# The first unit of a clustered-attention kernel: the second head's choice of clusters in pieces between the first steps

## The chip, the cores and the metric

One core of one Trainium2 chip runs the whole program. The time is that of the device for one execution, in microseconds (us); the kernel before was run three times and profiled once. TensorE is called PE, VectorE DVE, ScalarE ACT, GpSimd POOL; SP (SyncE) issues most transfers.

## What is computed

Attention in which a query sees only the keys of its own cluster, then a mixture of experts, then a dense layer, all in float32 with 2 x 8 heads, 768 positions and head size 64:

```python
q_assign = argmax(q_n @ c_n.T)          # 16 centroids for each head, rows normed
k_assign = argmax(k_n @ c_n.T)
mask = q_assign[:, :, :, None] == k_assign[:, :, None, :]
scores = scale * (q @ k.T); scores = where(mask, scores, -1e9)
attn = exp(scores - max) / (sum + 1e-9);  x = attn @ v
# mixture of experts: 1536 tokens, width 512, 8 experts of 1024
# dense: width 512 -> 2048 -> 512, h * sigmoid(1.702 h)
```

## The kernel before

The attention goes over 8 units (a batch and a pair of heads each). A unit has 12 steps: two heads of six blocks of 128 queries. The steps of all units make one list, and the loop over `i` emits them as a pipeline, in program order, which is the order that each engine keeps: scores of step i + 1 on PE (`emit_scores`, L425 and L426, four matmuls of 384 columns into a buffer `sp`, of which there are two) with their row maximum on DVE (L428), then the transposes of step i - 1 (`emit_pt`, six on PE at L442; ACT copies the high part, L446, DVE the low part, L447), a part of the product with V (L464, L465), and the exponential of step i + 1 on ACT (L434).

Float32 numbers are split into a high and a low part, so each score is a product of stacked rows: Q1 and X hold high parts twice and high with low, and Q2 and Z hold low and high parts in rows 0 to 63 and the one-hot cluster of each position in rows 64 to 79, with a large penalty. Scores of a head so need the choice of its clusters: a product with the centroids, a chain of maxima and comparisons, a transpose of the one-hot, and a copy into rows 64 to 79 of Q2 and Z.

For units 1 to 7 this preparation is cut into nine pieces, which `prep_pieces` returns and `plan_at` hangs on steps of the unit before: 0 and 1 transpose q of the two heads (L244, with the high part on ACT at L247 and the low on DVE at L248), 2 and 3 the same for k; 1 and 3 also issue the copies into the stacks on SP (L262, six of 192 KB each); 4 and 5 are the products with the centroids for q and k (L274, L275, reduced at L277), 5 also starts the choice, of which three instructions run on POOL (L293 to L295); 6 splits v on POOL; 7 ends the choice on DVE (L302, L303), ahead of the step's scores; 8 transposes the one-hots (L310), copies them on ACT (L312) and issues four copies on SP (L314, L315). These pieces, the output stage, and the one-hots of unit 0 use the one PSUM buffer `m` of `misc` once the loop is under way. `load_unit` fetches q, k and v of a pair (three transfers of 384 KB) into one of two buffers each.

Unit 0 has versions of its own. Ahead of the loop it chooses the clusters of head 0 (`first["clusters"]`, L351 and L352, twelve matmuls; `first["argmax"]`, L360 to L368, a generator of eight DVE instructions), puts its one-hots straight into Q2 and Z (`first_onehots`: twelve transposes at L380, then four copies at L383 to L386), and does head 1 later: its one-hots go by `first["second"]`, which is the piece 8 for head 1 alone (L310, L312, and two copies on SP). Head 1 is used from step 6. `keep_clock(n)` runs n matmuls of zeros (L135, 512 columns, bf16).

In SP's queue, as in the other engines', an instruction that waits holds those behind it.

Of the kernel before, what the change touches and what calls it, by code (L numbers as in the profile page):

```python
# [13 lines left out]
AF = mybir.ActivationFunctionType  # L14
ALU = mybir.AluOpType
# [12 lines left out]
BIG = float(2 ** 100)  # L28
# [10 lines left out]
def tile_t(j):  # L39

    return 2 * (j % 3) + j // 3
# [3 lines left out]
def attention_moe_ffn(ctx: ExitStack, tc: tile.TileContext, q, k, v, centroids, w_gate, w_og, w1, w2, w_in, w_out, out):  # L45
    nc = tc.nc
# [9 lines left out]
    pen_scale = const.tile([80, 1], F32, name="pen_scale")  # L56
    pen_bias = const.tile([80, 1], F32, name="pen_bias")
# [73 lines left out]
    def keep_clock(n):  # L131

        z = ps_s.tile([128, 2, 512], F32, name="sp", tag="sp")
        for m in range(n):
            nc.tensor.matmul(z[:, m % 2], idle[:, 0:128], idle, start=True, stop=True)  # L135

    def setup_first():
        nc.vector.memset(idle, 0.0)
        keep_clock(5)
        nc.sync.dma_start(out=craw, in_=centroids.rearrange("h c d -> (h c) d"))  # L140
        for h in range(2):
            load_unit(0, "q", h)
            load_unit(0, "k", h)
        make_identity(nc, ident)
        nc.vector.tensor_copy(identb, ident)
        ii = one.tile([128, C], I32, name="ii")
        nc.gpsimd.iota(ii, [[-1, C]], base=C, channel_multiplier=0)
        nc.vector.tensor_copy(rev16, ii)
        nc.vector.memset(pen_scale[0:32], 1.0)
        nc.vector.memset(pen_scale[32:64], BIG)  # L150
        nc.vector.memset(pen_scale[64:80], BIG)
        nc.vector.memset(pen_bias[0:32], 0.0)
        nc.vector.memset(pen_bias[32:64], -BIG)
        nc.vector.memset(pen_bias[64:80], -BIG)
# [21 lines left out]
    def setup_blocks(cnorm):  # L176
        pc = ps_a.tile([128, 512], F32, name="pc", tag="po")
        nc.tensor.transpose(pc[:, :128], cnorm.rearrange("p a d -> p (a d)"), ident)
        src = [pc[64 * r:64 * r + 64, :128].rearrange("p (h c) -> p h c", h=H) for r in range(2)]
        hi = [cblk[64 * r:64 * r + 64, :, r, :] for r in range(2)]  # L180
        for r in range(2):
            nc.scalar.copy(hi[r], src[r])
        for r in range(2):
            nc.vector.tensor_tensor(cblk[64 * r:64 * r + 64, :, 2 + r, :], src[r], f32(hi[r]), op=ALU.subtract)
# [32 lines left out]
    def misc(u, nm):  # L217

        pool, tag = spots[0]
        if len(spots) > 1:  # L220
            spots.append(spots.pop(0))
        return pool.tile([128, 512], F32, name=nm, tag=tag)

    def prep_pieces(u):
# [146 lines left out]
        def first_onehots():  # L371

            flat = d["oh"].rearrange("p t x c -> p (t x c)")
            pts = {}
            for x in (2, 0):
                pt = misc(u, "poh")[0:XW].bitcast(BF16)[:, 0:S]
                pts[x] = pt[64:80]
                for j in range(T):
                    end = (1 + tile_t(j)) * 4 * C + (x + 1) * C
                    nc.tensor.transpose(pt[:, j * 128:(j + 1) * 128], flat[:, end - XW:end], identb)  # L380
            a, b = slice(0, 384), slice(384, S)
            q2, z = d["Q2"][64:80, 0], d["Z"][64:80, 0]
            nc.vector.tensor_scalar(z[:, a], pts[2][:, a], BIG, -BIG, op0=ALU.mult, op1=ALU.add)  # L383
            nc.scalar.activation(z[:, b], pts[2][:, b], AF.Identity, scale=pen_scale[64:80], bias=pen_bias[64:80])
            nc.scalar.copy(q2[:, a], pts[0][:, a])  # L385
            nc.scalar.copy(q2[:, b], pts[0][:, b])  # L386

# [22 lines left out]
    def emit_scores(i):  # L410
        u, h, j = steps[i]
        d = st[u]
        L = live[i] = {}
        if j % 3 == 0:
            L["sm"] = pp.tile([128, 3], F32, name="sm", tag="sm")
            L["pth"] = ptp.tile([128, T, 384], F32R, name="pth", tag="pth")
            L["ptl"] = ptp.tile([128, T, 384], F32R, name="ptl", tag="ptl")
        else:
            for nm in ("sm", "pth", "ptl"):
                L[nm] = live[i - 1][nm]  # L420
        sp = L["sp"] = ps_s.tile([128, 2, 512], F32, name="sp", tag="sp")
        cs = slice(j * 128, (j + 1) * 128)
        for n in range(2):
            ks = slice(384 * n, 384 * n + 384)
            nc.tensor.matmul(sp[:, n, :384], d["Q1"][:, h, cs], d["X"][:, h, ks], start=True, stop=False)  # L425
            nc.tensor.matmul(sp[:, n, :384], d["Q2"][:, h, cs], d["Z"][:, h, ks], start=False, stop=True)  # L426
        nm = L["nm"] = pp.tile([128, 1], F32, name="nm", tag="nm")
        nc.vector.tensor_reduce(nm, sp[:, :, :384], op=ALU.max, axis=AX.XY, negate=True)  # L428

    def emit_exp(i):  # L430
        L = live[i]
        j = steps[i][2]
        P = L["P"] = pp.tile([128, 2, 384], F32, name="P", tag="P")
        nc.scalar.activation(P, L["sp"][:, :, :384], AF.Exp, bias=L["nm"], accum_out=L["sm"][:, j % 3:j % 3 + 1])  # L434
# [222 lines left out]

    plan_at = {}
    for u in range(1, len(UNITS)):
        for n, r in enumerate((-3, -2, 0, 1, 3, 4, 7, 6, 7) if u > 1 else (2, 2, 3, 3, 4, 5, 7, 6, 7)):  # L660
            plan_at.setdefault((12 * (u - 1) + r, n == 7), []).append((u, n))
    pieces = {}

    def prepare(i, early=False):
        for u, n in plan_at.get((i, early), ()):
            if u not in pieces:
                pieces[u] = prep_pieces(u)
            for f in pieces[u][n]:
                f()

    with tc.manual_schedule():
        setup_first()
        first = prep_pieces(0)
        cnorm = setup_centroids()
        first["tr"]("q", 0)()
        first["alloc"]()
        first["tr"]("k", 0)()
        setup_blocks(cnorm)
        first["stacks"](0, "q")()
        first["stacks"](0, "k")()  # L680
        load_unit(0, "v")
        first["tr"]("q", 1)()
        first["tr"]("k", 1)()
        sc = [first["clusters"](0)]
        load_unit(1, "qk")
        chain = [first["argmax"](0, sc[0])]
        for _ in chain[0]:
            pass
        sc.append(first["clusters"](1))
        keep_clock(2)  # L690
        chain.append(first["argmax"](1, sc[1]))
        for _ in range(4):
            next(chain[1])
        first["stacks"](1, "q")()
        first["stacks"](1, "k")()
        first["onehots"]()
        setup_rest()
        first["vsplit"]()
        load_unit(1, "v")
        emit_scores(0)  # L700
        emit_exp(0)
        for i in range(NS + 2):
            if i == 1:
                for _ in chain[1]:
                    pass
            nu, r = divmod(i + 3, 12)
            if i == 3 or r == 0 and nu + 2 < len(UNITS):
                load_unit(nu + 2)
            prepare(i, True)
            if i + 1 < NS:  # L710
                emit_scores(i + 1)
            tail = i >= NS - TAIL
            if (tail or i % 3 == 2) and ost:
                ost.popleft()()
            if i == 1:
                first["second"]()
            prepare(i)
            if i == 0:
                spots[:] = [(ps_m, "m")]
            if i >= 14 and i % 4 == 2 and len(fill) < E:  # L720
                zero_rows(len(fill))
            if i % (NS // 2) == NS // 2 - 5 and i < NS:
                sum_logits(i // (NS // 2))
            if i == NS // 2 + 13:
                routing.append(route(0))
            for _ in range(2 if tail else 1):
                if av:
                    av.popleft()()
            if 0 <= i - 1 < NS:
                emit_pt(i - 1)  # L730
            n = i - (1 if tail else 2)
            if 0 <= n < NS and steps[n][2] % 3 == 2:
                queue_av(n)
            if i + 1 < NS:
                emit_exp(i + 1)
        advance(stop="weighed")
        while av:
            av.popleft()()
        while ost:
            ost.popleft()()  # L740
        advance()
        routing.append(route(2))
        advance()
        finish_routing()
        keep_clock(24)
# [336 lines left out]
    with tc.manual_schedule():  # L1082
# [4 lines left out]
        z = ps_h.tile([128, 512], F32, name="ph", tag="ph")  # L1087
# [17 lines left out]
        for g in range(G + 2):  # L1105
            e, c = divmod(g, 8)
            nxt = wins.get(e + 1)
            r = c - (7 - nxt["nr"]) if nxt else 0
# [76 lines left out]
    with tc.manual_schedule():  # L1185
        gq = deque()
        for g in range(len(seq) + 2):
# [6 lines left out]
            if g >= 2:  # L1194

                for m in range(4) if g < len(seq) or g == len(seq) + 1 else ():
                    for g0, gh, gl in list(gq)[:1] if g < len(seq) else gq:
                        fh, tb, c, i = seq[g0]
# [47 lines left out]
```

## Time and profile before

| | us |
|---|---|
| median of three runs | 778.91 (778.26 to 782.12) |
| the profiled execution | 779.88, of which its span is 778.2 |
| busy PE | 738.0 (95%) |
| busy DVE | 516.3 (66%) |
| busy ACT | 427.4 (55%) |
| busy POOL | 272.7 (35%) |
| mean granted clock of PE | 0.977 of full |

The profile is one execution of the program. Busy times are sums over the whole of it, so they say which engine has most work, not what a stage waits for: for that one reads the same figures by stretches, and the timeline, which lists the instructions in order with the idle time ahead of each and what ended it. The clock is granted at two levels, 1.0 (2.4 GHz) and 0.5 (1.2 GHz); a figure between is a mean over a stretch with both. The attention takes the first 294 us or so of the span; the unit in question, unit 0, its first 55.

### The profile page before, as it was taken

What the parts mean: (1) busy time and instruction counts of PE and PEld (TensorE: products, weight loads), DVE (VectorE), ACT (ScalarE), POOL (GpSimd) and SP (SyncE); (2) the same over time, 40 slices, a digit from 0 to 9 for tenths busy, and PEclk for the clock granted to TensorE, in tenths of its full rate; (3) what the DMA queues carried; (4) which work ended last, traced back from release to release, by engine and by line L of the source; (5) the groups of instructions that cost most, each with busy time, mean ns of one, the idle gap of its engine ahead of it and who ended that gap; (6) DMA issues with size and microseconds to landing.
All of it is one profiled execution on the core that took longest, in us unless ns stands there. A gap on an engine that the chain in (4) does not pass through costs nothing. (4 is left out here: it accounts for less than half of the span.)

```text
span 778.2 us, 12334 instructions
## 1 busy us (share of the span) xinstructions
PE 738.0 (95%) x4355; PEld 653.9 (84%) x4356; DVE 516.3 (66%) x995; ACT 427.4 (55%) x880; POOL 272.7 (35%) x208
## 2 busy tenths in 40 slices
PE   7899999999999995999999999999999999999996
PEld 5789989898898983999989988877888888888885
DVE  6788988989998983445666676786755567342422
ACT  4576867778687861555767777553534335221221
POOL 7022020220372003565767888543521021110101
PEclk7899999999999997799999999999999999999999
DMA  6764749345261004966666876235631121010101
GB/s 167 174 167 143 208 128 274 112 104 132 75 179 33 1 1 154 332 215 207 197 215 219 268 240 222 67 77 104 82 80 55 54 80 56 0 55 1 54 1 54
DMA packets 64608, 97.05 MB, mean 125 GB/s; under 512 B 8832, under 2 KB 42880, under 8 KB 64544
## 3 DMA queue, kind: packets, MB, share of 16 engines
q1 hardware_dynamic: 62240, 89.94, 39.9%
q0 software_dynamic: 2304, 6.30, 2.2%
q8 instruction: 35, 0.57, 0.3%
q14 instruction: 29, 0.24, 0.1%
HBM read 64.46 MB, written 12.59 MB: 99 GB/s over the span
## 5 line engine op out<-in xcount | busy, mean ns | idle before, releaser
L798 POOL TENSOR_TENSOR w<-raw,w 128x1024 fp32r<-128x1024 f32 x47 | 117.5, 2514 | 28.0 <-ACT w L795 25.1
L447 DVE TENSOR_TENSOR ptl<-pt,pth 128x384 fp32r<-128x384 f32 x192 | 98.4, 550 | 24.1 <-ACT pth L446 22.8
L446 ACT CAST pth<-pt 128x384 fp32r<-128x384 f32 x192 | 83.4, 482 | 46.4 <-PE pt L442 45.0
L1153 DVE TENSOR_TENSOR sg<-ph,sg 128x512 f32<-128x512 f32 x48 | 33.2, 692 | 102.8 <-ACT sg L1152 97.3
L434 ACT ACTIVATE P<-sp,nm 128x768 f32<-128x768 f32 x96 | 87.8, 915 | 14.9 <-DVE nm L428 14.3
L428 DVE TENSOR_REDUCE nm<-sp 128x1 f32<-128x768 f32 x96 | 91.0, 948 | 3.2 <-PE sp L426 3.2
L856 POOL TENSOR_TENSOR w<-csq,w 128x512 fp32r<-128x512 f32 x32 | 43.5, 1360 | 136.9 <-ACT w L855 136.9
L1152 ACT ACTIVATE sg<-ph 128x512 f32<-128x512 f32 x48 | 28.6, 597 | 108.2 <-PE ph L1074 107.6
L442 PE MATMUL pt<-ident,P 128*128 128x128 f32 x576 | 82.3, 278 | 0.8 <-DVE ptl L447 0.7
L1170 PE MATMUL py<-w,gl 128*128 128x512 f32 x192 | 75.3, 392 | 2.4 <-DVE gl L1159 2.4
L1073 PE MATMUL ph<-ytl,w 128*128 128x512 f32 x192 | 76.1, 396 | 0.0
L1072 PE MATMUL ph<-yth,w 128*128 128x512 f32 x192 | 75.9, 395 | 0.0
L425 PE MATMUL sp<-X,Q 128*128 128x384 f32 x192 | 74.8, 389 | 0.8 <-ACT P L434 0.8
L1074 PE MATMUL ph<-yth,w 128*128 128x512 f32 x192 | 75.5, 393 | 0.0
L442 PEld LDWEIGHTS pt<-ident,P 128*128 128x128 f32 x576 | 68.5, 142 | 8.2 <-DVE ptl L447 4.8
L1169 PE MATMUL py<-w,gh 128*128 128x512 f32 x192 | 75.3, 392 | 0.0
L1168 PE MATMUL py<-w,gh 128*128 128x512 f32 x192 | 75.0, 391 | 0.0
L464 PE MATMUL po<-pth,vst 128*128 128x384 f32 x192 | 71.3, 371 | 0.0
L795 ACT CAST w<-raw 128x1024 fp32r<-128x1024 f32 x63 | 65.8, 1045 | 4.9 <-DMA raw<-in_moe_w_dram 4.8
L426 PE MATMUL sp<-Z,Q 80*128 80x384 f32 x192 | 66.8, 348 | 1.1 <-ACT Q L385 1.1
L906 PE MATMUL py<-ht,w 128*128 128x480 f32 (+5 forms) x192 | 61.2, 352 | 6.7 <-DVE room L913 4.5
L465 PE MATMUL po<-ptl,vst 128*128 128x384 f32 x192 | 64.8, 338 | 0.0
(232 smaller groups left out, 1746.2 us busy)
## 6 DMA issues: line engine op xcount, KB each, us to landing
raw<-in_moe_w_dram SPq DMA_DIRECT2D x64, 512.0 KB, 3.8
raw<-in_moe_w_in_dram SPq DMA_DIRECT2D x16, 512.0 KB, 3.9
raw<-in_moe_w_out_dram SPq DMA_DIRECT2D x16, 512.0 KB, 4.4
xd<-zrow SPq DMA_DIRECT2D x8, 768.0 KB, 6.4
Q<-Hq SPq DMA_DIRECT2D x28, 192.0 KB, 3.0
ld_v<-in_v_dram SPq DMA_DIRECT2D x8, 384.0 KB, 4.8
xr<-xd SPq DMA_DIRECT2D x6, 512.0 KB, 5.5
ld_q<-in_q_dram SPq DMA_DIRECT2D x7, 384.0 KB, 3.3
```

What stands on the lines that cost most here:

```text
L428: nc.vector.tensor_reduce(nm, sp[:, :, :384], op=ALU.max, axis=AX.XY, negate=True)
L434: nc.scalar.activation(P, L["sp"][:, :, :384], AF.Exp, bias=L["nm"], accum_out=L["sm"][:, j % 3:j % 3 + 1])
L442: nc.tensor.transpose(pt[:, r * 128:(r + 1) * 128], L["P"][:, n, r * 128:(r + 1) * 128], ident)
L446: nc.scalar.copy(hi, src)
L447: nc.vector.tensor_tensor(L["ptl"][:, 3 * n:3 * n + 3, qs], src, f32(hi), op=ALU.subtract)
L798: (eng or nc.gpsimd).tensor_tensor(lo, r, f32(hi), op=ALU.subtract)
L1072: nc.tensor.matmul(ph, wa(key, 0, k, i), yth[:, k, cs], start=(k == 0), stop=False)
L1073: nc.tensor.matmul(ph, wa(key, 0, k, i), ytl[:, k, cs], start=False, stop=False)
L1074: nc.tensor.matmul(ph, wa(key, 1, k, i), yth[:, k, cs], start=False, stop=(k == 3))
L1168: nc.tensor.matmul(po[m], gh[:, ms], wb(key, 0, i), start=first, stop=False)
L1169: nc.tensor.matmul(po[m], gh[:, ms], wb(key, 1, i), start=False, stop=False)
L1170: nc.tensor.matmul(po[m], gl[:, ms], wb(key, 0, i), start=False, stop=last)
```

## The change

Four edits. The copy of the second half of Z's one-hots of head 0 goes from ACT to DVE. The pieces of unit 1 move to other steps: 0 and 1 from step 2 to 1 and 2, 2 and 3 from step 3 to 4 and 5, 4 and 5 from 4 and 5 to 6 and 7, 6 from 7 to 9, 7 from 6 to 8, 8 from 7 to 9. Ahead of the loop the cluster matmuls of head 1, two matmuls of zeros and the first four instructions of head 1's choice give way to fourteen matmuls of zeros; the cluster matmuls come at i = 0 after the scores, and the eight instructions of the choice in twos, threes and fours (three are left for the last) behind the scores' maxima of i = 0, 1 and 2, in place of four ahead of the loop and four at i = 1. The one-hots of head 1 are sent at i = 3 instead of i = 1.

```diff
-            nc.scalar.activation(z[:, b], pts[2][:, b], AF.Identity, scale=pen_scale[64:80], bias=pen_bias[64:80])
+            nc.vector.tensor_scalar(z[:, b], pts[2][:, b], BIG, -BIG, op0=ALU.mult, op1=ALU.add)
...
-        for n, r in enumerate((-3, -2, 0, 1, 3, 4, 7, 6, 7) if u > 1 else (2, 2, 3, 3, 4, 5, 7, 6, 7)):
+        for n, r in enumerate((-3, -2, 0, 1, 3, 4, 7, 6, 7) if u > 1 else (1, 2, 4, 5, 6, 7, 9, 8, 9)):
...
         chain = [first["argmax"](0, sc[0])]
         for _ in chain[0]:
             pass
-        sc.append(first["clusters"](1))
-        keep_clock(2)
-        chain.append(first["argmax"](1, sc[1]))
-        for _ in range(4):
-            next(chain[1])
+        keep_clock(14)
         first["stacks"](1, "q")()
...
         for i in range(NS + 2):
-            if i == 1:
-                for _ in chain[1]:
-                    pass
             nu, r = divmod(i + 3, 12)
             if i == 3 or r == 0 and nu + 2 < len(UNITS):
                 load_unit(nu + 2)
             prepare(i, True)
             if i + 1 < NS:
                 emit_scores(i + 1)
+
+            if i == 0:
+                sc.append(first["clusters"](1))
+                chain.append(first["argmax"](1, sc[1]))
+            for _ in range((2, 3, 4)[i] if i < 3 else 0):
+                next(chain[1], None)
...
-            if i == 1:
+            if i == 3:
                 first["second"]()
             prepare(i)
```

## Rows read from the trace of the kernel before

**Rows 1.** The page's first part: busy time, share of the span, instructions.
```profile
PE 738.0 (95%) x4355; PEld 653.9 (84%) x4356; DVE 516.3 (66%) x995; ACT 427.4 (55%) x880; POOL 272.7 (35%) x208
```

**Rows 2.** Busy time by stretch: stretch and length, engines (instructions), granted clock, DMA, GB/s.
```profile
core 0: us, PE busy (x) PEld busy (x) DVE busy (x) ACT busy (x) POOL busy (x), PEclk, DMA share, GB/s
0.00:50.00 50.00, 40.92 (x233) 34.17 (x234) 35.32 (x81) 27.29 (x58) 20.67 (x50) 0.83 0.62 154
...
46.00:60.00 14.00, 14.00 (x102) 13.65 (x102) 13.45 (x27) 12.12 (x29) 0.00 (x0) 1.00 0.68 184
...
100.00:150.00 50.00, 48.41 (x344) 45.25 (x343) 45.56 (x86) 36.55 (x84) 11.26 (x10) 1.00 0.53 157
```

**Rows 3.** The same view where the granted clock changes.
```profile
8.70:9.00 0.30, 0.30 (x4) 0.30 (x4) 0.30 (x2) 0.00 (x0) 0.30 (x1) 0.53 0.39 92
...
22.30:22.50 0.20, 0.20 (x3) 0.20 (x3) 0.12 (x1) 0.08 (x2) 0.00 (x0) 0.82 0.00 0
...
28.00:30.00 2.00, 1.09 (x6) 1.09 (x7) 0.86 (x2) 0.41 (x2) 0.00 (x0) 0.80 0.95 204
...
32.60:32.80 0.20, 0.20 (x4) 0.20 (x3) 0.20 (x1) 0.00 (x0) 0.00 (x0) 0.97 1.04 277
```

**Rows 4.** Timeline, steps 1 to 3: start, length, engine, line, operation [idle before <-releaser].
```profile
18.54 0.69 PE L425 MATMUL sp<-X,Q 128*128 128x384 f32 x1 [0.79 <-ACT P L434]
18.66 0.57 DVE L366 TENSOR_TENSOR eq<-eq,rev 128x96 f32<-128x96 f32 x2
...
26.04 0.56 DVE L248 SCALAR_TENSOR_TENSOR Lq<-pqk,Hq 128x384 fp32r<-128x384 f32 x1 [1.17 <-ACT Hq L247]
...
26.52 1.01 DVE L447 TENSOR_TENSOR ptl<-pt,pth 128x384 fp32r<-128x384 f32 x2
```

**Rows 5.** Timeline: zeros at the two clocks, and the start up to the first maximum.
```profile
298.58 3.32 PE L135 MATMUL sp<-idle 128*128 128x512 bf16 x14
...
1.26 2.31 PE L135 MATMUL sp<-idle 128*128 128x512 bf16 x5 [1.26 <-DVE idle L138]
...
11.73 0.36 DVE L368 TENSOR_TENSOR oh<-eq,m 128x192 bf16<-128x192 f32 x1
...
13.45 0.56 DVE L383 TENSOR_SCALAR Z<-poh 16x384 fp32r<-16x384 bf16 x1
...
15.16 0.66 PE L426 MATMUL sp<-Z,Q 80*128 80x384 f32 x1 [1.10 <-ACT Q L385]
...
16.50 0.96 DVE L428 TENSOR_REDUCE nm<-sp 128x1 f32<-128x768 f32 x1 [2.50 <-PE sp L426]
```

**Rows 6.** Timeline of SP's queue: stack copies of unit 1's q, loads of unit 2.
```profile
27.47 0.59 SPq L262 DMA_DIRECT2D Q<-Lq  x1
...
32.21 0.45 SPq L124 DMA_DIRECT2D ld_v<-in_v_dram  x1
```

**Rows 7.** Issue to landing: one stack copy of 32.76; the one-hot copies (L314), min, median, max.
```profile
X<-Hk SPq DMA_DIRECT2D x1, 192.0 KB, 7.6
...
DMA to landing us min/median/max: 2.3/2.6/2.8
```

**Rows 8.** Timeline from the scores of step 6 to the transposes of step 8.
```profile
34.41 0.34 PE L426 MATMUL sp<-Z,Q 80*128 80x384 f32 x1
...
34.94 0.20 PE L274 MATMUL pcl<-cblk,Hk 128*128 128x64 f32 x1
...
36.20 0.42 PE L464 MATMUL po<-pth,vst 128*128 128x384 f32 x1
...
40.88 0.55 DVE L302 TENSOR_REDUCE m<-eq 128x24 f32<-128x384 f32 x1 [1.84 <-POOL eq L295]
...
42.09 0.52 PE L310 MATMUL poh<-identb,oh 128*64 128x128 bf16 x6 [1.51 <-DVE oh L303]
...
43.88 0.98 ACT L312 ACTIVATE ohT<-poh,pen_bias,pen_scale 64x768 fp32r<-64x768 bf16 x1
...
49.15 0.82 PE L442 MATMUL pt<-ident,P 128*128 128x128 f32 x6
```

## The prediction, made before the changed kernel had run

> **What bounds the kernel now.** I read the page first: TensorE is busy for 95% of the span [rows 1]. Then the busy time by stretch: from 46 us on PE works without a gap (14.00 of 14.00 us) and it stays near that through the attention (48.41 of 50), but in the first 50 us it works 40.92 at a mean clock of 0.83 [rows 2]. So a later start of the steady stretch moves the end one for one, and the change is worth what it does to the first unit. I then looked at the granted clock there: it falls from full (2.4 GHz) to half (1.2) at 8.70, while PE runs the short matmuls of the choice of clusters, comes back at 22.37, some 3.8 us after PE's score matmuls begin to follow closely at 18.54, falls again at about 29.2 and is back at 32.6 [rows 3, 4]. Last I followed the order on each engine in the timeline, because in the first unit nearly everything waits for something else, and SP's queue with the time each transfer takes to land [rows 5 to 8].
>
> I mark the end of the changed stretch by the second group of transposes of step 8 (emitted at i = 9): in the trace of before it ends at 49.15 + 0.82 = 49.97 [rows 8]. After that point both kernels have the same work left. What I look for is this mark in the changed kernel.
>
> **Part 1: the start.** Removed ahead of the first scores: the twelve cluster matmuls of head 1, two matmuls of zeros, and four DVE instructions of head 1's choice. Added: fourteen matmuls of zeros on PE from about 8.44, where head 1's cluster matmuls began. Fourteen of them took 3.32 us at full clock and five took 2.31 us at half, 0.46 each, so fourteen would take 6.5 at half [rows 5]. The transposes of head 0's one-hots wait for DVE's last instruction at 11.73 + 0.36 = 12.09 in any case [rows 5]. At full clock the zeros end at 11.8 and cost nothing, since DVE's chain of 3.5 us hides them; if that cover is gone, each 0.24 to 0.46 us shows. At half clock throughout they end at 14.9 and hold PE for 2.8 us. The work ahead of them is the same as before, so I let the clock fall at 8.70 again, and come back 3.8 us after dense work begins, at about 12.2, as it did at 22.37. By then nine are done; five at 0.24 end at 13.4. PE is 1.3 us late there, but now at full clock.
>
> From the one-hot transposes on: at full clock the first six take about 0.5 us with latency. DVE is free now (before, head 1's four instructions kept it until 13.45 [rows 5]); it writes both halves of Z, 0.56 each, 13.9 to 15.0, the second in place of ACT's. ACT starts at once on Q. The last first-step matmul then starts at about 15.0 and its row maximum at 15.4, against 16.50 before [rows 5]: 1.1 us gained, mostly because the score matmuls take 0.34 instead of 0.66 each [rows 5, 8].
>
> **Part 2: the choice of head 1 between steps 0 to 2, and q of the second pair one a step.** Here DVE is the chain. From the maximum of step 2, at 18.3, it has in order: maximum 0.95, three pieces of 0.28 to 0.36 (1.0), the low part of q's first head 0.56, two low parts of transposed scores 1.01, maximum 0.95, the last three pieces 1.0, the low part of q's second head 0.56 [rows 4, 5]: 6.0, with small gaps 6.2, so that low part ends at 24.5, against 26.04 + 0.56 = 26.60 before [rows 4]. This far the change is 2 us ahead.
>
> **Part 3: head 1's one-hots, moved from i = 1 to i = 3.** Every instruction of that call moves: six transposes, one ACT copy, and two transfers on SP. In before SP issues these two ahead of the six stack copies of the second pair's q and the three loads of the third pair. Now `load_unit(2)` at the head of i = 3 and the stacks of i = 2 are ahead of them. In before the seven issues from the first low-part copy to the last load take from 27.47 to 32.66, 5.2 us [rows 6]. In the changed kernel the first low-part copy can be issued at 24.5, hence the one-hot rows at 24.5 + 5.2 = 29.7, though ACT has them ready at about 26. SP's issue is what is late, and behind it the scores of step 6, the first of head 1, which need these rows; every later PE instruction is queued behind that matmul, and PE reaches it at about 28.
>
> When do they land? With nothing ahead such a copy takes 2.3 to 2.8 us [rows 7]: 32.4 at best. In before the copy X<-Hk, issued at this very place behind the same nine transfers, took 7.6 us [rows 7]: 37.3 at worst. I take 6.0, nearer to that row, since the place in the queue is the same and only the size is smaller: 35.7.
>
> No row shows a one-hot copy behind long transfers, only copies of 192 KB. The Trainium skill, page "DMA: Bandwidth & Descriptors", section "Two DMAs through the same engine are not ordered", says that within one queue of one DMA engine descriptors start in order; by that rule a small copy cannot pass, and the sum goes with the 7.6 rather than the 2.8. It speaks against this move.
>
> **Part 4: from the scores of step 6 to the mark.** In before this took from 34.41 to 49.97, 15.6 us [rows 8]. In the changed kernel three things are added. (a) k's second transposes (about 0.3) and the cluster matmuls of q, 34.94 to 36.20 for such a set, 1.3 [rows 8], have moved behind this point: 1.6 us of PE. (b) PE has been idle from 28 to 35.7, so the clock will have fallen as it did at 8.70 and 29.2 [rows 3], and when work begins it is half for some 3.8 us: 1.9 us of work lost (0 if it holds). (c) The second pair's one-hots now come at i = 9, the same step as the third pair's first q transposes, and both use the one PSUM buffer `m`. The second must wait for ACT's copy of 0.98, which itself stands behind the exponential of step 9, which waits for the maximum that stands behind DVE's wait for POOL (1.84 before [rows 8]). In before PE waited 1.51 us there and had a step's work between; now it waits some 2.9 us more than it works: I put 1.4 on top. Here DVE's wait for POOL is unchanged, one step apart as before. Sum: 15.6 + 1.6 + 1.9 + 1.4 = 20.5.
>
> The mark: 35.7 + 20.5 = 56.2 against 49.97, so 6.2 us later.
>
> **Edits that I cost at nothing.** The load of the fourth pair's v at i = 9 now precedes the POOL split that reads the old v, so SP waits for POOL, with the one-hot copies of the second pair queued behind. ACT's copy for these comes after that anyway, and two steps lie before their use; if that cover is gone it costs 0 to 5 us (7.6 less 2.8 [rows 7]); I take 0, for the range up to 2. The cluster matmuls of head 1 at i = 0 lie beside DVE's maxima.
>
> **The rivals.**
> Rival A, the small copies pass the long ones: 32.4 in place of 35.7, hence +2.9 us, 781.8; with the clock held, +1.0, 779.9. For it: they are a quarter of the size. Against: the 7.6 and 2.8 of [rows 7] differ by the queue ahead.
> Rival B, on the faster side: the scores of step 6 are not held at all, because the issue of the nine transfers runs ahead of my order, and the clock then holds. PE starts them at 28: 28 + 15.6 + 1.6 + 1.4 = 46.6, 3.4 us earlier, 775.5; without (c) 774.1. The point from which it turns is a landing before 31.4. Against it: SP's own issue takes until 29.7.
> Rival C, the zeros do not do what they are for: the clock stays at half while they run and after. PE is held to 14.9 and runs the first transposes and scores at half: 2.4 us on top of the forecast, 787.5. For it: the two zeros of before did not bring the clock back until 22.37 [rows 3].
>
> **How the numbers follow.** The profiled execution took 779.88 us with a span of 778.2; the median of three runs is 778.91. Plus 6.2 on the median is 785.1. Half a per cent, about what a measurement of this kernel can tell from no change, is 3.9 us: 775.0 to 782.8. Chances: forecast 0.55, A 0.20, B 0.13, C 0.12. Slower than 782.8: nearly all of the forecast (0.50) and C, some of A when the one-hot copies of the second pair are late too: 0.62. Faster than 775.0: most of B, 0.11. The rest, 0.27, within. The range leaves out B and the edge of C: 777.5 to 790.0.
>
> **What would show it.** Part 1: the granted clock back near 12, the first maximum near 15.4. Part 2: the second low part of q ending near 24.5. Part 3: SP issues Q<-ohT of head 1 after the three loads, near 29.7, landing over 5 us later; the longest idle time of PE in the first 50 us stands at step 6, released by that transfer, and the clock falls in it. Part 4: the mark near 56, and steady PE work from there. The forecast is wrong if PE has no gap at step 6, if the copies land within 3 us, or if the mark lies before 50.

## The result and the profile after

The changed kernel takes 786.73 us (median of five, 786.33 to 787.82) against 780.65 for the kernel before in the same runs (778.26 to 782.12): a ratio of 1.0084, with a 95% interval of 1.0061 to 1.0108. It is 6.1 us slower; 6.2 had been forecast, from the 778.91 us that before had taken then. The profiled execution has a span of 784.6 us, 6.4 more than before.

The busy time by stretch (the columns of [rows 2]) shows where: the first 50 us hold 37.71 us of PE work where they held 40.92, and from 46 us on, where PE had no gap before, it now has 3.2 us of them. The six short stretches are those in which the granted clock changes, as in [rows 3]: down, up, down, up, down, up.

```profile
core 0: us, PE busy (x) PEld busy (x) DVE busy (x) ACT busy (x) POOL busy (x), PEclk, DMA share, GB/s
0.00:50.00 50.00, 37.71 (x224) 29.72 (x224) 30.95 (x76) 24.08 (x52) 18.63 (x49) 0.90 0.62 162
46.00:60.00 14.00, 10.84 (x73) 10.27 (x71) 9.16 (x21) 8.78 (x20) 5.82 (x5) 0.88 0.24 70
8.30:8.50 0.20, 0.20 (x3) 0.20 (x3) 0.00 (x0) 0.00 (x0) 0.20 (x1) 0.56 0.26 62
11.60:11.80 0.20, 0.20 (x2) 0.04 (x1) 0.04 (x1) 0.00 (x0) 0.20 (x1) 0.66 1.31 361
32.20:32.40 0.20, 0.00 (x0) 0.00 (x0) 0.00 (x0) 0.00 (x0) 0.00 (x0) 0.54 1.02 361
39.00:39.40 0.40, 0.40 (x5) 0.40 (x4) 0.00 (x0) 0.31 (x1) 0.00 (x0) 0.95 0.90 211
52.40:52.80 0.40, 0.00 (x0) 0.00 (x0) 0.40 (x2) 0.40 (x2) 0.00 (x0) 0.87 0.00 0
56.00:56.20 0.20, 0.20 (x3) 0.20 (x2) 0.00 (x0) 0.00 (x0) 0.00 (x0) 0.73 0.18 46
```

The mean clock of the first 50 us has risen from 0.83 to 0.90: it comes back at about 11.7, while the zeros run and before the first scores. But it falls again near 32.2, when PE has done nothing since 27.7, and near 52.7.

The timeline of the changed kernel tells the rest. The first lines answer to [rows 4] and [rows 5], the SP lines to [rows 6], the last to [rows 8].

```profile
8.38 4.84 PE L135 MATMUL sp<-idle 128*128 128x512 bf16 x14
...
13.05 0.83 PE L380 MATMUL poh<-identb,oh 128*80 128x128 bf16 x12
...
15.29 1.82 DVE L428 TENSOR_REDUCE nm<-sp 128x1 f32<-128x768 f32 x2 [0.68 <-PE sp L426]
...
23.38 0.55 DVE L248 SCALAR_TENSOR_TENSOR Lq<-pqk,Hq 128x384 fp32r<-128x384 f32 x1
...
23.96 0.59 SPq L262 DMA_DIRECT2D Q<-Lq  x1
...
24.52 0.99 ACT L312 ACTIVATE ohT<-poh,pen_bias,pen_scale 64x768 fp32r<-64x768 bf16 x1 [0.85 <-PE poh L310]
...
28.92 0.58 SPq L314 DMA_DIRECT2D Q<-ohT  x1
29.55 0.58 SPq L315 DMA_DIRECT2D Z<-ohT  x1
35.19 0.66 PE L426 MATMUL sp<-Z,Q 80*128 80x384 f32 x1 [7.49 <-DMA Z<-ohT]
...
49.33 0.55 DVE L302 TENSOR_REDUCE m<-eq 128x24 f32<-128x384 f32 x1 [1.77 <-POOL eq L295]
...
51.72 0.49 PE L310 MATMUL poh<-identb,oh 128*64 128x128 bf16 x6 [2.01 <-DVE xw L483]
...
53.36 0.90 PE L244 MATMUL pqk<-ident,ld_q 128*128 128x128 f32 x3 [1.15 <-ACT ohT L312]
...
55.34 1.19 PE L442 MATMUL pt<-ident,P 128*128 128x128 f32 x6
```

The issue-to-landing times of the last load and the two one-hot copies (KB, us), as in [rows 7]:

```profile
ld_v<-in_v_dram SPq DMA_DIRECT2D x1, 384.0 KB, 6.3
...
Q<-ohT SPq DMA_DIRECT2D x1, 48.0 KB, 5.9
...
Z<-ohT SPq DMA_DIRECT2D x1, 48.0 KB, 5.5
```

What to see: the one-hot transposes of head 0 start 0.9 us later than before (13.05 against 12.14), behind the zeros, but from the first maximum up to 24 us everything is earlier (the first maximum by 1.2 us, the low part of q's second head, which ended at 26.60, by 2.7). ACT has head 1's one-hots ready at 25.5. SP issues them at 28.92 and 29.55, behind the six stack copies and three loads, and they land 5.9 and 5.5 us later, at 34.8 and 35.1, just behind the last load (28.39 + 6.3 = 34.7); one matmul of PE waits 7.49 us for them. The mark (end of step 8's transposes) lies at 56.53 against 49.97, 6.56 later, and the last output matmuls of the attention begin at 297.76 against 291.17, 6.59 later: between them nothing was won back.

### The profile page after: what moved, and what is told of

It is laid out like the page before. It is cut to its first block, busy times and chain, and to the rows that moved or that the text cites. A ratio compares the mean times of both kernels' runs of the same rounds, so it can differ in the third digit from the quotient of the medians.

```text
span 784.6 us, 12359 instructions
## 1 busy us (share of the span) xinstructions
PE 738.9 (94%) x4368; PEld 653.2 (83%) x4368; DVE 515.7 (66%) x996; ACT 427.4 (54%) x879; POOL 272.4 (35%) x208
## 5 line engine op out<-in xcount | busy, mean ns | idle before, releaser
L797 POOL TENSOR_TENSOR w<-raw,w 128x1024 fp32r<-128x1024 f32 x47 | 117.2, 2507 | 27.6 <-ACT w L794 24.8
L447 DVE TENSOR_TENSOR ptl<-pt,pth 128x384 fp32r<-128x384 f32 x192 | 98.3, 550 | 25.3 <-ACT pth L446 24.5
L425 PE MATMUL sp<-X,Q 128*128 128x384 f32 x192 | 73.1, 381 | 0.1
```

The lines of the kernel that those rows point to most:

```text
L447: nc.vector.tensor_tensor(L["ptl"][:, 3 * n:3 * n + 3, qs], src, f32(hi), op=ALU.subtract)
L797: (eng or nc.gpsimd).tensor_tensor(lo, r, f32(hi), op=ALU.subtract)
```

## The experiments

Theory: the scores of step 6 wait for head 1's one-hot rows because the call that sends them stands behind nine transfers in SP's queue; its issue and its landing are both late for that. Rivals: the small copies are late for another reason; the loss lies in the pieces that moved behind step 6 and in the one buffer `m`; the zeros do harm.

All times are medians; "before", run beside each, was 780.2 to 780.7 us. The last three columns come from the one profiled execution of each kernel. The copy of Z that went from ACT to DVE was not tried by itself.

| kernel | us | first maximum | step 6 released (before: starts) | mark |
|---|---|---|---|---|
| before | 780.65 | 16.50 | 34.41 | 49.97 |
| changed | 786.73 | 15.29 | 35.19 | 56.53 |
| copies on ACT's queue | 780.87 | 14.44 | 29.30 | 48.85 |
| loads behind the copies | 782.21 | 14.45 | 29.74 | 50.62 |
| nothing ahead of them | 777.98 | 14.41 | 28.23 | 48.06 |
| two zeros | 789.19 | 15.61 | 37.40 | 58.81 |
| nothing ahead, two zeros | 781.07 | 16.29 | 31.51 | 51.35 |
| before, the call moved alone | 785.42 | 17.33 | 39.03 | 56.30 |
| zeros in the gap | 785.17 | 15.31 | 34.92 | 53.20 |

### The call moved alone, in the kernel before

```diff
-            if i == 1:
+            if i == 3:
                 first["second"]()
```

> The kernel before (780.6 us) with one thing altered: head 1's one-hots are sent at i = 3 in place of i = 1, nothing else. Theory (place in SP's queue): the two copies are issued behind the same nine transfers, near 32.7, land 5.5 to 7 us later, near 39; step 6's scores, which began at 34.41, begin near 39, the clock falls in the gap, the time 785 to 788. Rival (the loss comes with the other edits): 780 to 782.

785.42 us, ratio 1.0065 (1.0044 to 1.0086): this one line is worth 5.1 of the 6.1 us. SP issues the copies at 32.91 and 33.55, behind the same nine transfers, and step 6 is released at 39.03. The gap in front of it is only 1.0 us, less than expected: in before the clock fell at about 29.2 and was back at 32.6; here it falls at about 29.8 and PE works through the clusters at half pace up to the waiting matmul; it comes back only at 46.6. Why it stays down so long is not shown. So the loss shows as slow work more than as idle time. The timeline of this run:

```profile
32.91 0.58 SPq L314 DMA_DIRECT2D Q<-ohT  x1
33.55 0.58 SPq L315 DMA_DIRECT2D Z<-ohT  x1
...
39.03 0.66 PE L426 MATMUL sp<-Z,Q 80*128 80x384 f32 x1 [1.00 <-DMA Z<-ohT]
```

### Nothing ahead of the copies

```diff
-            for f in pieces[u][n]:
+            for f in pieces[u][n][:1 if (u, n) == (1, 1) else None]:
...
-            if i == 3 or r == 0 and nu + 2 < len(UNITS):
+            if r == 0 and nu + 2 < len(UNITS):
                 load_unit(nu + 2)
...
             if i == 3:
                 first["second"]()
+                pieces[1][1][1]()
+                load_unit(2)
```

`pieces[1][1][1]` issues the stack copies of the second pair's q; piece 1 itself keeps only its transposes, at i = 2.

> The changed kernel with the six stack copies of q and the three loads of the third pair emitted behind the one-hot copies of head 1 at i = 3; all else as in the changed kernel. Theory (place in SP's queue): issue near 25.6, landing 2.3 to 2.8 later, near 28.3; no gap over 0.5 us at step 6, the clock stays at full there, the mark near 47 to 48, the time 777 to 779, at or a little under the kernel before (780.65 in the same runs' spread of 778 to 782). Rival (the loss is in the pieces moved behind step 6 and the buffer m): time 783 or more.

777.98 us, ratio to before 0.9957 (0.9937 to 0.9977): with the order in SP's queue mended and nothing else, the changed kernel is 8.7 us faster and beats the kernel before by 0.4%. The copies are issued at 25.30 and 25.94 and land in 2.1 and 2.2 us; PE waits 0.76 us at step 6. The timeline of this run:

```profile
25.30 0.59 SPq L314 DMA_DIRECT2D Q<-ohT  x1
25.94 0.59 SPq L315 DMA_DIRECT2D Z<-ohT  x1
...
28.23 0.41 PE L426 MATMUL sp<-Z,Q 80*128 80x384 f32 x1 [0.76 <-DMA Z<-ohT]
```

And its wait view around step 9 (who waited for whom, total, times, longest):

```profile
PE poh L310 <- DVE xw L483: 2.0, 1, 2.0
PE pqk L244 <- ACT ohT L312: 1.2, 1, 1.2
```

The rival that the loss lies in the moved pieces and the buffer is out as the main cause; its two waits at step 9 are still there in this faster kernel.

### The loads behind the copies, the stacks ahead

```diff
-            if i == 3 or r == 0 and nu + 2 < len(UNITS):
+            if r == 0 and nu + 2 < len(UNITS):
                 load_unit(nu + 2)
...
             if i == 3:
                 first["second"]()
+                load_unit(2)
```

> The changed kernel with the three loads of the third pair emitted behind the one-hot copies of head 1 at i = 3, in place of ahead of them; the six stack copies of q stay ahead. Theory (place in SP's queue): issue of the first one-hot copy near 26.6 instead of 28.9, with half of the bytes ahead; landing near 31 to 32 instead of 35.2. The gap at step 6 falls from 7.5 to 3 to 4 us, the time to 781 to 783. If issue alone matters and the bytes ahead do not: landing 2.8 after issue, 29.5 to 30, time 779 to 781. If neither matters: 786 to 787.

782.21 us; the copies are issued at 25.87 and 26.61 and land in 3.1 and 3.0 us, near 29.7. That is earlier than the 31 to 32 that the theory gave: the stack copies were issued over 4.6 us, and three of the six had landed when the second one-hot copy was issued; the last lands at 28.5 (25.15 + 3.3), the one-hots at 29.0 and 29.6. So of the 5.9 us of landing behind all nine, some 2.8 belong to the three loads, issued just ahead, and 0.9 to the six stacks. The gap on PE is 2.79 us, and behind it the clock falls: it is 0.50 from 32 to 34. Of the 4.2 us by which this kernel's median lies above that with nothing ahead, the marks of the two profiles account for 2.6 (50.62 against 48.06); the rest is not shown.

```profile
30.00:31.00 1.00, 1.00 (x8) 0.97 (x8) 0.46 (x1) 0.13 (x1) 0.00 (x0) 1.00 1.03 375
31.00:32.00 1.00, 1.00 (x7) 0.91 (x6) 0.97 (x2) 0.37 (x1) 0.00 (x0) 0.65 0.95 286
32.00:33.00 1.00, 1.00 (x6) 1.00 (x5) 0.18 (x1) 0.54 (x2) 0.00 (x0) 0.50 0.80 273
```

### The copies on ACT's queue

```diff
-        def onehots(heads=(0, 1)):
+        def onehots(heads=(0, 1), q_=None):
+            q_ = q_ or nc.sync
...
-                nc.sync.dma_start(out=f32(d["Q2"][64:80, h]), in_=f32(ot[C * h:C * h + C]))
-                nc.sync.dma_start(out=f32(d["Z"][64:80, h]), in_=f32(ot[32 + C * h:32 + C * h + C]))
+                q_.dma_start(out=f32(d["Q2"][64:80, h]), in_=f32(ot[C * h:C * h + C]))
+                q_.dma_start(out=f32(d["Z"][64:80, h]), in_=f32(ot[32 + C * h:32 + C * h + C]))
...
-                        onehots=first_onehots, vsplit=vsplit, second=lambda: onehots((1,)))
+                        onehots=first_onehots, vsplit=vsplit, second=lambda: onehots((1,), nc.scalar))
```

> The changed kernel (786.7 us) with one thing altered: the two copies of head 1's one-hots at i = 3 are issued by ACT, on a queue of its own, instead of SP; order and work on PE, DVE and POOL are the same. Theory (place in SP's queue): the copies are issued near 25.6, as soon as ACT has them, and land in about 3 us, near 29, because the long transfers stand in another queue. PE's gap of 7.5 us at step 6 shrinks to 0 to 2, the clock does not fall there, the mark (end of step 8's transposes, 56.5 in the changed kernel) comes to 48, and the time to 778 to 780. Rival (the transfers share the engines whatever the queue, and the copies wait for their bytes): landing stays near 33 to 35, the time 784 to 787. Rival (the loss is in the pieces moved behind step 6 and the buffer m): the gap shrinks but the time stays above 784.

780.87 us. ACT issues the copies at 24.79 and 25.46, when SP has issued five of its nine (the sixth at 25.16) and none of the loads (the first at 25.86), and they land in 3.5 and 3.7 us: step 6 is released at 29.30. What the other queue gives is the earlier issue, 24.8 for 28.9. It does not show that a copy lands faster for standing in another queue: with the loads behind the copies in SP's own queue, the run above, they landed in 3.1 and 3.0 us behind the same six stack copies. The rival of shared engines forecast a landing at 33 to 35, which did not come; the step from the 2.1 of a clear queue to 3.6 is what it can be worth. The time is 0.9 above what was expected: ACT spends 1.3 us on issuing, its copy of the scores' high part starts behind that, and PE waits 1.53 us for the low part that follows.

```profile
24.79 0.62 ACTq L315 DMA_DIRECT2D Q<-ohT  x1
25.46 0.67 ACTq L316 DMA_DIRECT2D Z<-ohT  x1
26.17 0.86 ACT L447 CAST pth<-pt 128x384 fp32r<-128x384 f32 x2 [1.41 <-PE pqk L244]
...
27.30 1.01 PE L443 MATMUL pt<-ident,P 128*128 128x128 f32 x6 [1.53 <-DVE ptl L448]
29.30 0.41 PE L427 MATMUL sp<-Z,Q 80*128 80x384 f32 x1 [0.82 <-DMA Z<-ohT]
```

### Two zeros in place of fourteen

```diff
-        keep_clock(14)
+        keep_clock(2)
```

> The changed kernel with two matmuls of zeros ahead of the first scores in place of fourteen. Theory (the start is worth 1 us, but what sets step 6 is SP's queue, which hangs on DVE's chain): the one-hots of head 0 start at 12.1 instead of 13.05 but at half clock, which then stays until the work is dense; first maximum 0 to 1 us later than 15.29, step 6 released 0 to 2 us later, the time 786.5 to 789. If the fourteen zeros are only a load on PE: 1 us faster, 785.5. If they are what keeps the whole first unit fast: 790 or more.

789.19 us, 2.5 more than the changed kernel and just past the end of the theory's range. The clock is half from 13 to 23 (0.50 in both stretches), the first maximum is 0.3 later and the low part of q 2.4 later, which moves the whole queue on SP by that much. So the zeros, which hold PE 0.9 us too long in the changed kernel, give 2.5 back.

The same edit on top of those of the kernel with nothing ahead of the copies:

> The run with nothing ahead of head 1's one-hot copies (777.98 us), with two matmuls of zeros in place of fourteen. Theory (the zeros are worth what DVE's chain gains, and step 6 hangs on that chain): with two zeros in the changed kernel the transposes of head 1's one-hots started at 26.36 against 23.98, 2.4 us later, so step 6 is released 2.4 later here too: 780 to 781, and the clock stays at half until about 22. If step 6 has slack once the queue is clear: 778.

781.07 us, 3.1 more than with fourteen. Step 6 is released 3.3 us later, of which 0.7 had already been lost at the first transposes. The zeros' worth does not hang on the queue.

### Zeros in the gap

```diff
+            if i == 5:
+                keep_clock(26)
             if i + 1 < NS:
                 emit_scores(i + 1)
```

> The changed kernel (786.73 us) with 26 matmuls of zeros ahead of the scores of step 6, in the gap of 7.5 us in which PE waits for the one-hot copies: about 5.7 us of work at full clock that nothing waits for. It parts the gap itself from the clock that falls in it. Theory: the copies land at 35.2 as before, the clock stays at full, PE's work from there runs in half the time for the first 3.5 to 4 us: 1.5 to 2 us faster, 784.7 to 785.2. If the clock behind the gap costs nothing (DVE and ACT bound there): 786.7.

785.17 us, 1.6 less than the changed kernel, from runs that spread from 783.1 to 787.7 (there 786.3 to 787.8); the ratios to before, 1.0057 (1.0029 to 1.0085) and 1.0084 (1.0061 to 1.0108), overlap, so the medians alone do not settle that it is faster. In its profile the copies release step 6 at 34.92, as late as in the changed kernel, but the clock is at full throughout 23 to 64, and the mark lies at 53.20 instead of 56.53: 3.1 us less from release to mark (18.28 against 21.34).

```profile
34.92 0.42 PE L426 MATMUL sp<-Z,Q 80*128 80x384 f32 x1 [1.60 <-DMA Z<-ohT]
```

The busy time by stretch, at the release and at step 9:

```profile
34.00:40.00 6.00, 5.08 (x37) 5.00 (x38) 3.77 (x6) 2.25 (x5) 0.00 (x0) 1.00 0.33 76
46.00:52.00 6.00, 2.84 (x23) 2.43 (x22) 4.09 (x7) 2.86 (x6) 3.91 (x4) 1.00 0.11 30
```

This parts the bill of a profiled execution: the two falls of the clock behind the gaps cost about 3 us of the mark, the late copies alone what is left. The second fall, at step 9, stays away here although no zeros stand there and PE waits the same 2.01 and 1.16 us: with the same waits it comes in one execution and not in another.

### The third pair's transposes late, and the choice spread

Both go on from the kernel with nothing ahead. The first moves one piece within step 9:

```diff
-            plan_at.setdefault((12 * (u - 1) + r, n == 7), []).append((u, n))
+            plan_at.setdefault((12 * (u - 1) + r, "late" if (u, n) == (2, 0) else n == 7), []).append((u, n))
...
                 emit_pt(i - 1)
+            prepare(i, "late")
```

The second has these lines too, spreads the choice over steps 7, 8 and 9 (the tuple of the steps of the second pair's pieces), and moves the fourth pair's loads from i = 9 to i = 10:

```diff
-            if r == 0 and nu + 2 < len(UNITS):
+            if r == 0 and nu > 1 and nu + 2 < len(UNITS):
                 load_unit(nu + 2)
+            if i == 10:
+                load_unit(3)
...
-(1, 2, 4, 5, 6, 7, 9, 8, 9)
+(1, 2, 4, 5, 6, 7, 8, 9, 9)
```

> The run with nothing ahead of the one-hot copies (777.98 us), with the third pair's first q transposes moved within step 9 from ahead of the product with V to behind the step's transposes. Theory (part 4 (c): two users of the one buffer m in one step): PE's wait of 1.2 us for ACT's one-hot copy goes, that of 2.0 us for the output stage stays; PE idles less, so the clock falls behind it less often: 1 to 2.5 us faster, 775.5 to 777. Rival (DVE sets the pace there): 778.

> As the run with the late transposes, and the end of the second pair's choice at the head of step 9 in place of 8 (two steps behind its start, as for the other pairs), its split of v at step 8, and the loads of the fourth pair at i = 10 behind the one-hot copies. Theory: DVE's wait of 1.8 us for POOL at step 8 goes, and with it PE's wait of 2.0 us for the output stage behind it: 774 to 776. Rival (the one-hots come too late for step 12, with the row copies issued near 45): a new wait of 1 to 2 us at the scores of step 12, 777 to 779.

777.73 and 777.53 us: both within 0.5 us of the 777.98 they started from, and at 0.9958 (0.9932 to 0.9984) and 0.9963 (0.9944 to 0.9983) of before. Neither is distinguishable from its base. In the first PE's wait for ACT's one-hot copy is gone, but PE waits twice, 1.5 us in all, for the low part of the third pair's q; in the second DVE's wait for POOL is gone too, but then PE waits 2.71 us for the one-hots themselves, which come later:

```profile
45.24 0.52 PE L310 MATMUL poh<-identb,oh 128*64 128x128 bf16 x6 [2.71 <-DVE oh L303]
```

The waits at steps 8 and 9 are one chain over DVE, POOL, ACT and the buffer; a link taken out lets the next one come last.

A third, also on top of the kernel with nothing ahead, was meant to give 3 to 5 us:

```diff
-(1, 2, 4, 5, 6, 7, 9, 8, 9)
+(1, 2, 3, 4, 5, 6, 8, 8, 8)
```

> The run with nothing ahead of the one-hot copies (777.98 us), with the second pair's pieces 2 to 8 at steps 3, 4, 5, 6, 8, 8 (ahead of its scores) and 8 in place of 4, 5, 6, 7, 9, 8 and 9: the start of the choice is two steps ahead of its end, and the one-hots are a step ahead of the third pair's first transposes. Theory (part 4's stall by POOL and by the one buffer m is worth what PE idles at i = 9): the waits of 2.0 and 1.2 us on PE there go, and the clock does not fall behind them: 3 to 5 us faster, 773 to 775. Rival (DVE and ACT are full in these steps and the idle time moves elsewhere): 777 to 779.

It gave 779.57 us, 1.6 more than its base, at 0.9981 (0.9963 to 0.9999) of before: the gain did not come, and whether it is slower than its base the overlapping intervals leave open. Two new conflicts for `m` were put in: the first k transposes now wait 1.1 us for ACT's copy at i = 3, with the clock falling behind it (0.64 in 23 to 28), and the one-hots stand behind the output stage in the same step, 2.2 us.

## Why the prediction was right

**The start** was right in its parts, one slip aside. The zeros ended at 13.22 (13.4 forecast), the clock came back at about 11.7 while they ran (12.2), and the first maximum began at 15.29 (15.4). The slip: from 8.44 to 12.2, at 0.46 each, eight zeros are done, not nine, and the rest would end at 13.6.

That this course came was luck: in the profiles of several experiments the zeros ran at full clock throughout (3.20 us for the fourteen) and the first maximum came at 14.4 to 14.6; in that of the choice spread they began only at 9.86, ran at half pace until about 13, and it came at 16.65. The forecast's single course is one of three. Nor do the 3.8 us after which the forecast let the clock come back hold elsewhere: with the call moved alone PE worked from 30.50 with one gap of 1.0 us, and the clock was at half until 46.6.

**DVE's chain** ended at 23.93 (24.5). The last step of the choice did fit between the maxima, and no engine stood in its way.

**The call moved behind the queue** was right in place and size: issue at 28.92 (29.7), release of step 6 at 35.19 (35.7). The landing of 5.5 to 5.9 lies where it was put (6.0), between the 2.8 of a clear queue and the 7.6 of a large copy behind the nine. (29.7 + 2.8 is 32.5, where 32.4 was written.) In SP's queue the copies landed in 5.9 and 5.5 us behind nine transfers, 3.1 and 3.0 behind six, 2.1 and 2.2 behind none, and where transfers stood ahead they landed behind the last of these. That rival A did not happen is thereby shown: here the copies do not pass. The Trainium skill, page "DMA: Bandwidth & Descriptors", section "Two DMAs through the same engine are not ordered", says that descriptors of one queue start in order on an engine, but not that they end so. The order that was measured, the last load at 34.7 and the copies at 34.8 and 35.1, agrees.

**From step 6 to the mark** the forecast was 20.5 and the trace shows 56.53 - 35.19 = 21.34. The half clock behind the gap lasts from the release to about 39.04, 3.85 us (3.8 forecast), so 1.9 of work lost. Two things were off. A second fall, at 52.7 to 56.1, was not in the sum; PE works from 53.36 in it, 2.7 us, so 1.4 lost. And in (c) one wait of some 2.9 us was written, behind ACT's copy; the trace has two, 3.2 us together. The first, 2.01 us of the one-hot transposes, is for DVE's scaling of the output stage of step 8 (xw), which uses the same `m` and stands behind DVE's wait for POOL, and was not seen; the 1.15 for ACT's copy was. The 1.4 us put on top for (c) come out smaller: with (a) at the 1.6 that was written, 21.34 less 15.6, 1.6, 1.9 and 1.4 leaves 0.9 for it, and the run with zeros in the gap, where the clock did not fall, 18.28 less 15.6 and 1.6, so 1.1 (estimates). What (c) would give back is not shown: the two kernels that took its waits apart gained under 0.5, but other waits took their place.

That 6.2 and 6.1 agree to 0.1 is luck in that measure: the release came 0.5 us early, and the stretch behind it took 0.8 more.

**After the mark** the loss went through one for one, 6.56 at the mark and 6.59 at the last output stage.

**The rivals.** C, that the clock would stay at half, was priced at 2.4 us; the run with two zeros, where it does up to 24 us, is 2.5 slower; it has not C's fourteen slow zeros, so the agreement is a near one. B, the faster side, needed step 6 not to be held: the kernel with nothing ahead is nearly that, released at 28.23 (28 was written). It is 2.6 us faster than before in the same runs, where 3.4 was written. Its mark lies at 48.06 instead of 46.6: the clock fell behind the waits at step 9 (0.62 in 46 to 52), which B's sum did not hold. The rest of the way from the 775.5 that was written to 777.98 is before itself, 780.60 in these runs and 778.91 then.

## What to carry to other kernels

When a call is moved to a later step, list what else its queue holds between the old place and the new one: an instruction that takes its engine no time can hand a small copy to the back of megabytes. Copies that a next step waits for go ahead of loads that nothing waits for yet; here their order in one queue was worth 8.7 us. A gap on TensorE is to be priced with the half-rate work that may stand behind it: the clock fell at the gaps of 7.49 and 2.79 us, and stayed at full at one of 2.71 (the choice spread). And a wait in a chain over several engines is to be priced with the link that comes last when it is gone.

## What the runs showed of the hardware

The granted clock in the records can be wrong until its first change. In the run with the call moved alone the view gives 1.00 for 8.4 to 13 and 13 to 18, but the score matmuls follow each other at 0.32 us, the pace that they have in the changed kernel at 35.65, where the view gives 0.50, and not at the 0.18 of its 39.45, where it gives 1.00. The busy time by stretch:

```profile
8.40:13.00 4.60, 4.60 (x21) 4.00 (x22) 2.97 (x10) 0.00 (x0) 4.27 (x9) 1.00 0.82 234
13.00:18.00 5.00, 4.01 (x20) 3.64 (x20) 2.40 (x6) 1.40 (x3) 4.49 (x22) 1.00 0.82 201
```

The timeline of the same run:

```profile
16.45 0.52 PE L425 MATMUL sp<-X,Q 128*128 128x384 f32 x1
16.77 0.52 PE L426 MATMUL sp<-Z,Q 80*128 80x384 f32 x1
```

So in that execution the clock had not come up by then, and its first maximum came at 17.33 where the profile of before has 16.50. The choice spread shows the same: its view gives 1.00 for 8.4 to 13, where six zeros took 2.74 us, 0.46 each. The pace of the matmuls is the check. From one execution to the next the clock takes different courses in the first 20 us, with the same instructions ahead of it; that moved the start by 0.8 us here, and by up to 2.2 with fourteen zeros (14.41 to 16.65). It may be part of why the kernel before spreads from 778 to 787 us; that is not shown. Of a gain or loss under 1 us nothing can therefore be read from one trace.

A copy of 48 KB lands in 2.1 us from a clear queue, in 3.0 to 3.1 behind six copies of 192 KB and in 5.0 to 5.9 behind these and three loads of 384 KB (2.3 MB) in its own queue (the changed kernel, the two zeros, the zeros in the gap). In the two profiles that were followed it landed 0.1 to 0.5 us behind the last of them. From ACT's queue, with SP's transfers in flight and the loads issued after it, it took 3.5 to 3.7: the bytes of the other queue count too, and no run here shows that the other queue by itself makes it land faster.
